# The last four gate and value tiles of blocks 3 to 8 as seven half-size products in place of eight

## The chip, the cores and the metric

The kernel runs on one core of one Trainium2 chip. The metric is the time of one execution on the device in microseconds (us). Executions of one kernel mostly agree within a few tenths of a per cent, so a ratio of two kernels is taken over several runs of each. One run of the kernel before, 349.77 us, is 1.6% above the fastest of its kernel, counts as slow and is left out of the ratio. A profile is one execution among these: its span is about 1.8 us shorter than the time reported for the same execution. Its opening (blocks 0 to 2 and the first loads) differs by up to 3 us. Parts of two profiles are therefore compared from block to block here, not by their spans.

## The reference

Two layers in a row. The first is a normed linear attention without softmax:

```
kv  = einsum('bhsd,bhse->bhde', k, v)          # batch 8, heads 8, rows 576, head size 64
out = einsum('bhsd,bhde->bhse', q, kv)
x   = out / sqrt(mean(out * out, -1) + 1e-6) * g_norm
```

The second is a gated feed-forward layer on the 4608 rows of x, each 512 wide:

```
h   = gelu(x @ w_gate) * (x @ w_val)           # 512 -> 1536
y   = x + sigmoid(x @ w_res) * (h @ w_out)     # 1536 -> 512
```

## The kernel before

Each batch of 576 rows gives a block of 512 rows, and the 64 rows left of each of the eight batches make the ninth block: blocks 0 to 8. While block m runs through the feed-forward layer, attention of batch m + 1 is slipped in between its tiles. Per block TensorE computes twelve pairs of tiles (gate and value, each four matmuls of 512 columns), then the residual gate, then the output product. The output product is already done as seven half-size products for eight (Strassen's scheme in Winograd's form), with the sums of `hid` (the h of the formulas) on VectorE; `wA` to `wF` are its accumulators. The order of instructions on each engine is set by this program.

The accumulators lie in PSUM, eight of 128x512 in fp32, called banks here, in two rings of four: `pmoe` for the feed-forward layer and `pattn` for attention.

```python
    pmoe = ctx.enter_context(tc.tile_pool(name="pmoe", bufs=4, space=bass.MemoryType.PSUM))
    pattn = ctx.enter_context(tc.tile_pool(name="pattn", bufs=4, space=bass.MemoryType.PSUM))
    ...
    def m_act(blk, f, gps, vps):
        ge = moep.tile([P, NJ * P], FP16, tag="ge", name="ge")
        nc.scalar.activation(out=ge, in_=gps, func=AF.Gelu)
        nc.vector.tensor_tensor(out=hids[blk][:, f, :], in0=ge, in1=vps, op=ALU.mult)
    ...
    def m_gval(blk, f, pool=pmoe, tag="mm"):
        ...
        gps = pool.tile([P, NJ * P], FP32, tag=tag, name="gps")
        m_mm(gps, wg_c, f, blk, 0, NJ)          # four matmuls of 512 columns
        vps = pool.tile([P, NJ * P], FP32, tag=tag, name="vps")
        m_mm(vps, wv_c, f, blk, 0, NJ)
        m_act(blk, f, gps, vps)
```

Attention's output `op` takes all four banks of `pattn`. ScalarE squares it, VectorE sums the squares (`a_ss`), then comes the norm (`a_norm`, twelve small instructions on VectorE: three refining steps of an inverse root), and `a_t` multiplies the four banks by it, which sets them free one by one:

```python
    def a_t(b, i):
        o, rinv = st[b]["o"][i], st[b]["rinv"]
        ...
        nc.vector.tensor_tensor(out=t, in0=o, in1=scale, op=ALU.mult)
```

Where these stand is set by numbers of tiles: `k0` for the product of keys and values, `o0` for the output, `n0` for the norm.

```python
        else:
            at(m - 1, NF, lambda: by_token(b, "q"))
            at(m - 1, NF + 1, lambda: by_token(b, "k"), *begin)
            k0, o0, n0 = 1, 3, 7
        at(m, k0, lambda: a_kv(b))
        ...
        at(m, o0, lambda: a_o(b))
        for j in range(NJ):
            at(m, o0 + j // 2, lambda j=j: a_ss(b, j))
        at(m, n0, lambda: a_norm(b, 0, NJ + rem))
        n0 += 1 if b == 2 else 2
        for j in range(NJ):
            at(m, NF if b == 2 and j > 1 else n0 + j // 2, lambda j=j: a_t(b, j))
```

## Time and profile before

| | before |
|---|---|
| time, median | 344.67 us (3 runs: 344.24, 344.67 and the slow 349.77) |
| span of the profile, of an execution of 347.15 us | 345.4 us |
| TensorE busy | 331.9 us, 96% |
| VectorE, ScalarE, GpSimd busy | 68%, 43%, 30% |
| waits of TensorE in blocks 3 to 8 | none listed |

The line of busy times says which engine is the bound; the list of waits of that engine says whether it loses anything to others. Here it loses next to nothing after the opening. The prediction below shows these lines and reads them.

### The profile page before, as it was taken

To read this page: it belongs to the slowest core of one execution; us is meant where nothing else is said; L and a number is where in the kernel's file an instruction comes from. 1 tells how busy PE (TensorE), PEld (TensorE's weight loads), DVE (VectorE), ACT (ScalarE), POOL (GpSimd) and SP (SyncE) were. 2 spreads that over 40 slices of the span, in tenths; PEclk is the share of its full clock that TensorE was granted. 3 is DMA by queue.
4 is the path that set the end of the run, shared out by engine and by line. 5 is a ranking of instruction groups with operands and counts; after the bars stand their busy time and mean duration, and the time that the engine had idled before them with its cause. 6 is when DMAs were issued, how large, how long until landed. Compare 5 with 4: busy or idle time off the path is not lost.

```text
span 345.4 us, 6165 instructions
## 1 busy us (share of the span) xinstructions
PE 331.9 (96%) x2432; PEld 188.0 (54%) x2432; DVE 236.5 (68%) x446; ACT 150.1 (43%) x265; POOL 103.1 (30%) x121
## 2 busy tenths in 40 slices
PE   8789999999899999999999999999999999999992
PEld 3544454445744475447544764476447644764481
DVE  5665549769859987698578976885688735453643
ACT  3573384274336352535263615361736133623350
POOL 2692161980064108200820083005000600050013
PEclk9899999999999999999999999999999999999997
DMA  7999999669589263966395439744003120030004
GB/s 244 290 178 204 195 204 166 168 95 150 117 108 164 94 123 120 165 60 128 130 167 43 102 114 174 79 92 153 17 0 61 63 76 2 1 121 4 0 2 121
DMA packets 76399, 38.81 MB, mean 112 GB/s; under 512 B 42066, under 2 KB 73810, under 8 KB 76370
## 3 DMA queue, kind: packets, MB, share of 16 engines
q0 software_dynamic: 38752, 17.17, 40.1%
q1 hardware_dynamic: 37184, 20.71, 21.6%
q10 hardware_dynamic: 434, 0.52, 0.5%
q8 instruction: 19, 0.31, 0.4%
q14 instruction: 10, 0.08, 0.1%
HBM read 38.80 MB, written 9.44 MB: 140 GB/s over the span
## 4 chain that ended last, share of the span: by engine, by line
PE 69%; DVE 2%; issue 0%; POOL 0%; POOLq 0%; DVEq 0%
PE gps L336 21%; PE vps L336 20%; PE wA L431 10%; PE rps L356 6%; PE wF L431 3%; PE wD L431 2%; PE w L431 2%; PE wE L431 2%; PE kvp L187 1%; PE op L205 1%; DVE t L282 1%; DVE hid L325 1%; DVE hid_s L404 0%; DVE t L296 0%; POOL osb L526 0%
## 5 line engine op out<-in xcount | busy, mean ns | idle before, releaser
L324 ACT ACTIVATE ge<-gps 128x512 f16<-128x512 f32 x108 | 64.3, 597 | 133.1 <-PE gps L336 127.8
L325 DVE TENSOR_TENSOR hid<-ge,vps 128x512 f16<-128x512 f16 x108 | 73.8, 684 | 63.2 <-PE vps L336 60.8
L336 PE MATMUL vps<-xT,wv 128*128 128x512 f16 x424 | 108.8, 379 | 0.4 <-DVE hid L325 0.4
L336 PE MATMUL gps<-xT,wg 128*128 128x512 f16 x424 | 109.0, 379 | 0.0
L470 POOL TENSOR_TENSOR osb<-osb,t 128x512 f32<-128x512 f32 x28 | 36.1, 1309 | 155.6 <-DVE osb L466 148.6
L336 PEld LDWEIGHTS <-wv 128*128 128x128 f16 x424 | 41.5, 98 | 50.6 <-issue 0.7
L336 PEld LDWEIGHTS <-wg 128*128 128x128 f16 x424 | 40.2, 98 | 45.4 <-issue 0.4
L431 PEld LDWEIGHTS <-hid_s 128*128 128x128 f16 x384 | 37.5, 98 | 6.3 <-issue 1.4
L356 PE MATMUL rps<-wr,xT 128*128 128x512 f16 x144 | 32.7, 379 | 0.0
L431 PEld LDWEIGHTS <-hid 128*128 128x128 f16 x288 | 28.2, 98 | 5.1
L365 ACT ACTIVATE th<-rps 128x512 f32<-128x512 f32 x36 | 21.5, 597 | 19.0 <-PE rps L356 19.0
L356 PEld LDWEIGHTS <-xT 128*128 128x128 f16 x144 | 14.1, 98 | 16.8
L224 DVE TENSOR_REDUCE ss<-sq 128x8 f32<-128x512 f32 x32 | 20.6, 679 | 2.9 <-ACT sq L222 2.7
L431 PE MATMUL wA<-wo_ts,hid_s 128*128 128x256 f16 x168 | 20.6, 273 | 1.2 <-DVE wF L404 1.2
L370 ACT ACTIVATE th<-th 128x512 f32<-128x512 f32 x36 | 19.9, 622 | 0.0
L282 DVE TENSOR_TENSOR t<-op,ny 128x512 f16<-128x512 f32 x28 | 17.9, 682 | 0.1
L222 ACT ACTIVATE sq<-op 128x512 f32<-128x512 f32 x28 | 15.3, 597 | 4.5 <-PE op L205 4.2
L296 DVE TENSOR_TENSOR t<-t,g 128x512 f16<-128x512 f16 x36 | 16.2, 498 | 0.1
L404 DVE TENSOR_TENSOR hid_s<-hid 128x1536 f16<-128x1536 f16 x16 | 15.3, 955 | 0.3
L526 POOL TENSOR_TENSOR osb<-osb,t 128x512 f32<-128x512 f32 (+1 forms) x4 | 4.3, 1078 | 27.8 <-DVE osb L522 27.8
L373 PE MATMUL fps<-wo,hid 128*128 128x512 f16 x48 | 11.2, 379 | 0.0
L431 PE MATMUL wD<-wo_ts,hid_s 128*128 128x256 f16 x84 | 10.3, 273 | 0.1
(133 smaller groups left out, 326.5 us busy)
## 6 DMA issues: line engine op xcount, KB each, us to landing
out_dram<-osb SPq DMA_DIRECT2D x14, 512.0 KB, 2.6
qraw<-in_q_dram POOLq DMA_DIRECT2D x7, 512.0 KB, 8.2
kraw<-in_k_dram POOLq DMA_DIRECT2D x7, 512.0 KB, 9.9
v<-in_v_dram POOLq DMA_DIRECT2D x7, 512.0 KB, 11.9
out_dram<-osb SPq DMA_DIRECT2D x5, 256.0 KB, 2.8
wg<-in_moe_w_gate_dram POOLq DMA_DIRECT2D x2, 512.0 KB, 9.2
wv<-in_moe_w_val_dram POOLq DMA_DIRECT2D x2, 512.0 KB, 9.4
wo<-in_moe_w_out_dram POOLq DMA_DIRECT2D x2, 512.0 KB, 14.2
```

Of the source, the lines that this page charges most:

```text
L222: nc.scalar.activation(out=sq, in_=src, func=AF.Square)
L224: nc.vector.tensor_reduce(out=out_, in_=sq, op=ALU.add, axis=mybir.AxisListType.X)
L282: nc.vector.tensor_tensor(out=t, in0=o, in1=scale, op=ALU.mult)
L296: nc.vector.tensor_tensor(out=t_t[blk][:, jj, :], in0=t_t[blk][:, jj, :], in1=g16, op=ALU.mult)
L324: nc.scalar.activation(out=ge, in_=gps, func=AF.Gelu)
L325: nc.vector.tensor_tensor(out=hids[blk][:, f, :], in0=ge, in1=vps, op=ALU.mult)
L336: nc.tensor.matmul(ps[:, j0 * P : j1 * P], lhsT=w[:, cc, :], rhs=xT_t[blk][:, j0:j1, cc, :], start=(cc == 0 and j0 == 0), stop=(cc == NP - ...
L356: nc.tensor.matmul(rps, lhsT=xT_t[blk][:, j, cc, :], rhs=wr16[:, cc, :], start=(cc == 0), stop=(cc == NP - 1),)
L365: nc.scalar.activation(out=th, in_=rps, func=AF.Tanh, scale=0.5)
L370: nc.scalar.activation(out=th, in_=th, func=AF.Copy, scale=0.5, bias=0.5)
L431: nc.tensor.matmul(ps[:, e - es[0], :], lhsT=a[:, f, e * P : (e + 1) * P], rhs=b[:, f, :], start=(start and e == es[0] and f == 0), stop=( ...
L470: nc.gpsimd.tensor_tensor(out=res_all[of], in0=res_all[of], in1=t_t[blk][of], op=ALU.add)
```

## The change

The intent: the last four pairs of tiles of a block, 512 rows by 512 deep by 512 columns for gate and for value, are done by the same scheme of seven half-size products in place of eight. TensorE is the bound, so an eighth of that part should be time saved. The two groups of 128 columns run side by side: for each, the accumulators `E` and `D` lie in `pmoe` and `A` in `pattn`, and the partial results set aside (`d`) in a buffer that is free at that time. The sums of the weights are taken once, in block 0, on VectorE; the sums of x per block on GpSimd. To clear attention's banks in time, the norm of batches 4 to 7 is moved from tile 7 to tile 5; the multiplication by g and one sum of `hid` move behind the products. Three buffers in SBUF were merged or cut to make room.

The core of the diff (cut):

```diff
+    def gval_by_products(blk):
+        ...
+        def prod_w(ps, g, a, b, start):
+            for n in range(2):                       # gate, value
+                for c in range(NP // 2):
+                    nc.tensor.matmul(ps[:, n, :], lhsT=a(n)[:, c, g * P : (g + 1) * P], rhs=b[:, :, c, :], ...)
+        def first():
+            for g in range(2):
+                w[g]["E"] = pmoe.tile([P, 2, PR], FP32, tag="mm", name="gE")
+                w[g]["D"] = pmoe.tile([P, 2, PR], FP32, tag="mm", name="gD")
+                w[g]["A"] = pattn.tile([P, 2, PR], FP32, tag="at", name="gA")
+                w[g]["d"] = th_all[:, g, :].rearrange("p (n t) -> p n t", n=2)
+                prod_w(w[g]["A"], g, wh(1, 1), x_of(blk, 1, 1), True)
+                nc.scalar.copy(out=w[g]["E"], in_=w[g]["A"])
+            for g in range(2):
+                prod_w(w[g]["D"], g, s_(1), x_sum[:, 0], True)
+                nc.scalar.copy(out=w[g]["d"], in_=w[g]["D"])
+        ... second, third, fourth: five more products, recombined by VectorE into D and c,
+        ... then gelu on ScalarE and the multiplication on VectorE (for c on GpSimd)
@@ plan_attn
-            k0, o0, n0 = 1, 3, 7
+            k0, o0, n0 = 1, 3, 5 if b > 3 else 7
-        n0 += 1 if b == 2 else 2
+        n0 += 1 if b != 3 else 2
-            at(m, NF if b == 2 else n0 + 1, lambda j=j: a_x(b, j))
+            at(m, n0 + 1 if b == 3 else NF, lambda j=j: a_x(b, j))
@@ blocks
+            if blk > 2:
+                slots[F0:] = gval_by_products(blk)
+                plan.setdefault(0, []).insert(0, lambda: x_sums(blk))
-            plan.setdefault(NFH + 2, []).insert(0, lambda: s_begin(blk))
+            if blk <= 2:
+                plan.setdefault(NFH + 2, []).insert(0, lambda: s_begin(blk))
             def products(blk=blk, outs=outs):
                 s_rest(blk)
+                if blk > 2:
+                    s_begin(blk)
```

## The prediction

> **What bounds the kernel now.** I read the page's busy shares first, then the costliest groups, then the waits of TensorE alone, and last the timelines of TensorE, VectorE and GpSimd over one steady block.
>
> From the page:
>
> ```profile
> PE 331.9 (96%) x2432; PEld 188.0 (54%) x2432; DVE 236.5 (68%) x446; ACT 150.1 (43%) x265; POOL 103.1 (30%) x121
> L325 DVE TENSOR_TENSOR hid<-ge,vps 128x512 f16<-128x512 f16 x108 | 73.8, 684 | 63.2 <-PE vps L336 60.8
> L282 DVE TENSOR_TENSOR t<-op,ny 128x512 f16<-128x512 f32 x28 | 17.9, 682 | 0.1
> ```
>
> TensorE (PE) is busy 96% of a 345.4 us span; the gate and value tiles wait almost only for it. All waits of TensorE that the profile lists are short, and none falls in blocks 3 to 8:
>
> ```profile
> PE kvp L718 <- DVE v L689: 2.5, 2, 2.3
> PE wA L431 <- DVE wF L404: 1.2, 1, 1.2
> PE vps L336 <- DVE hid L325: 0.4, 1, 0.4
> ```
>
> The windows of three such blocks show no idle time at all: 35.24, 34.86 and 34.50 us long, with PE busy for the whole of each at a granted clock of 1.00. So a us of products saved is a us of time saved, if nothing new makes TensorE wait. Its timeline in the block that starts at 201.64 us gives the rates (start, duration, columns as in the page; starts, not ends, tell the rate):
>
> ```profile
> 199.02 1.47 PE L431 MATMUL wF<-wo,hid_s 128*128 128x256 f16 x12
> 200.33 1.47 PE L431 MATMUL wA<-wo_ts,hid 128*128 128x256 f16 x12
> ...
> 211.81 1.03 PE L336 MATMUL gps<-xT,wg 128*128 128x512 f16 x4
> 212.67 1.03 PE L336 MATMUL vps<-xT,wv 128*128 128x512 f16 x4
> ...
> 216.99 1.03 PE L336 MATMUL gps<-xT,wg 128*128 128x512 f16 x4
> ...
> 223.89 2.32 PE L356 MATMUL rps<-wr,xT 128*128 128x512 f16 x10
> ```
>
> From 216.99 to 223.89 are the last four tile pairs: 32 matmuls of 512 columns in 6.90 us, 0.216 us each. Twelve of 256 columns start 1.31 us apart as a group (199.02 to 200.33), 0.109 us each. VectorE in the same block:
>
> ```profile
> 212.08 0.69 DVE L325 TENSOR_TENSOR hid<-ge,vps 128x512 f16<-128x512 f16 x1 [0.23 <-PE vps L336]
> 212.68 1.27 DVE L224 TENSOR_REDUCE ss<-sq 128x8 f32<-128x512 f32 x2
> 213.87 0.68 DVE L325 TENSOR_TENSOR hid<-ge,vps 128x512 f16<-128x512 f16 x1
> ...
> 217.86 0.17 DVE L254 TENSOR_SCALAR nm<-ss 128x32 f32<-128x32 f32 x1
> ...
> 220.10 0.19 DVE L262 SCALAR_TENSOR_TENSOR ny<-na,ny 128x32 f32<-128x32 f32 x1
> 220.21 0.68 DVE L325 TENSOR_TENSOR hid<-ge,vps 128x512 f16<-128x512 f16 x1
> ```
>
> The twelve small instructions of the norm take 220.21 - 217.86 = 2.35 us in a row, more than a pair of tiles on TensorE (1.73 us). Now that costs nothing: a late `hid` only holds a bank of a ring of four.
>
> **What the Trainium skill says.** "TensorE: Matmul & The Clock Gate", section "Wait — 56ns, not 53.3ns?", gives 215.7 ns from start to start at 512 columns, warm, as columns over 2.4 GHz plus 2.5 ns; for 256 that is an estimate of 109 ns. The trace has 216 and 109, so half-size products cost half and no more. "PSUM — Partial Sum Buffer", section "PSUM bank collisions raise a hardware error", says that two engines must not be in one bank and quadrant at once and that software has to guard it by semaphores; "Engine vs sequencer instructions" there says that VectorE's queue is strict FIFO. Together they are my main worry: a product may wait for a bank whose last reader sits behind the norm. The trace shows both: banks wait for `hid`, and VectorE keeps program order. "SBUF — State Buffer", section "Who interferes with whom", says that VectorE and GpSimd share a port pair as an exclusive lock, for a VectorE instruction with two SBUF inputs too. The trace agrees: one `t<-t,g` took 1.26 us at 203.42 beside a GpSimd addition, against four in 1.42 us at 190.46.
>
> **The change part by part.** Products: per block 32 x 0.216 = 6.90 us go, and 7 products x 2 groups x 4 matmuls = 56 x 0.109 = 6.12 us come: 0.78 us saved, 4.7 us over six blocks. That is the most it can give, 1.4%.
>
> Weight sums, once, in block 0: eight VectorE sums of 128x512 f16, about 0.34 us each (a 128x1536 one takes 0.955), 2.7 us. They delay the last `hid` of that block from 41.52 to about 43.1; its bank is wanted by the fourth residual product about 43.85. Hidden, narrowly.
>
> Token sums: four GpSimd sums at 1.3 us (the row of wo_ts) after the last block's additions, so from about 4.0 to 9.2 us of the block; wanted at 17. Hidden. The next loads are issued 5 us later, and have till about 30 us. Hidden.
>
> Pieces after the products (copies, recombining, gelus, multiplications): more instructions, half as large, on ScalarE (43% busy), VectorE and GpSimd. I laid them out by hand with 0.4 us for 256 columns and 0.69 for 512: once started, the fourteen group-products never wait longer than 0.2 us, since each bank is left for about 1.5 us between two uses.
>
> Start of the products: here I see the loss. The two `A` accumulators take attention's banks, whose last readers are the `t<-op,ny` multiplications. The order of instructions in the changed kernel shows two separate waits for VectorE in front of the two `A`; by rotation of four banks they are the first two `t`. The change brings the norm forward to behind tile 5, and the first two `t` behind tile 6. In the block above, by VectorE's own times: `hid` 5 at 213.87, norm from 214.47 to 216.82, `hid` 6, then the first `t` from 217.42 to 218.10. TensorE is ready at 216.99 and waits 1.15 us; the second `t` ends at 218.70 and costs 0.16 more. With the 6.12 us of products the phase ends near 224.4, against 223.89: 0.5 us worse than before. In blocks with remainder rows one more reduction (0.68 us) and a norm of 2.42 us come first: the first `t` ends near 184.0 where TensorE is ready at 182.13 in the block that starts at 166.40, a wait of 1.85 us, so 1.3 us worse. Blocks 3 and 5 are of the first kind, 4 and 6 of the second, and 7 and 8 have no attention, so they gain the full 0.75.
>
> End of the phase: the sums of `hid` for the output products begin about 1.8 us after the last product, as all four now come at the end, with the four `t<-t,g` and the next batch's two copies behind them. `wF<-wA,wd` then starts about 8.3 us after the last gate product, against 7.7 (196.67 - 189.01) before, and ends just after product E (8.7): a new wait of 0.1 to 0.4 us in blocks 3, 4 and 5, together 0.9. The transposed x of the next block is issued about 7.5 us after the phase, lands 4.3 us later (the trace's landing time) and is wanted at 12.6: hidden.
>
> Sum: 2 x 0.5 + 2 x 1.3 - 2 x 0.75 + 0.9 = +3.0 us, on 344.67: 347.7. VectorE may be a little quicker than laid out, and the change was made by someone who moved the norm on purpose, so I say 347.0.
>
> **The rivals.** First, the banks are free in time and the products save their 4.7 us: 340. For it: the norm was moved forward for just this, and blocks 7 and 8 have it. Against it: VectorE's timeline, where reductions, norm and two `hid` stand ahead of the first `t` with no idle time. Second, VectorE becomes the bound in the whole block (27.40 us of 34.86 now, some 1.5 us more): blocks grow by 1 to 2 us each at the end of the phase also, 350 to 352. Against it: 6 us idle remain. Third, GpSimd is late: its sums or its two multiplications are slowed by the shared port, or loads pushed back delay VectorE's copies; 349 or more. Against it: about 8 us of slack for the first sum, and GpSimd is 30% busy.
>
> **Range and chances.** The low end, 341.5, is nearly the full gain; the high end, 350.5, is twice my loss. Over 2% faster would need 337.8, beyond the most that the products can save. Over 2% slower needs 351.6, which takes the second rival in full.
>
> **What would show it.** Right: in blocks 3 to 6 the first `gA` waits 1 to 2 us for VectorE's `t`, longer in 4 and 6; the pieces within the phase run without gaps; blocks 7 and 8 are 0.75 us shorter; `wA` or `wF` of the output products waits a little for `wF<-wA,wd`. Wrong: no wait at the first `gA` (then 340), a wait for `x_sum` or the GpSimd `hid`, or 256-column products further apart than 0.11 us.

## The result, and the profile after

| | before | after |
|---|---|---|
| time, median of 4 runs each | 344.60 us (344.52 without the slow 349.77) | 348.06 us (347.30 to 348.77) |
| ratio, 95% interval | | 1.0104 (1.0075 to 1.0132) |
| TensorE busy | 331.9 us | 327.5 us |
| VectorE busy | 236.5 us | 251.2 us |
| GpSimd busy | 103.1 us | 137.5 us |

The output is correct.

TensorE has less work and the kernel is slower, by 1.0%. The page after, busy times:

```profile
PE 327.5 (95%) x2576; PEld 200.3 (58%) x2576; DVE 251.2 (73%) x490; ACT 164.9 (48%) x313; POOL 137.5 (40%) x157
```

The 4.4 us less of TensorE's busy time only look like what the products should save. From the residual products of block 2 to those of block 8 the busy time fell by 3.2 us, from 207.10 to 203.89; the rest is mostly in the opening, where the profile before had its 3.4 us at half the clock. The waits of TensorE in the changed kernel (in total, times, longest; those in the opening left out) say where the gain went:

```profile
PE gA L476 <- DVE t L283: 6.0, 4, 1.8
PE wA L432 <- DVE wF L405: 1.2, 1, 1.2
PE vps L337 <- DVE hid L326: 0.4, 1, 0.4
```

The last two were there before. The first is new: four waits of the first `gA` for `t`, attention's multiplication. Its 6.0 us against 3.2 us less of busy time make the 2.8 us that the blocks lose below. TensorE's timeline in block 5, which begins at 201.19 us, shows one; the brackets give the idle time ahead of an instruction and who ended it:

```profile
214.81 1.03 PE L337 MATMUL gps<-xT,wg 128*128 128x512 f16 x4
215.67 1.03 PE L337 MATMUL vps<-xT,wv 128*128 128x512 f16 x4
217.94 0.39 PE L476 MATMUL gA<-xT,wg 128*128 128x256 f16 x2 [1.24 <-DVE t L283]
218.17 0.38 PE L476 MATMUL gA<-xT,wv 128*128 128x256 f16 x2
218.53 0.39 PE L476 MATMUL gA<-xT,wg 128*128 128x256 f16 x2
...
221.60 1.04 PE L476 MATMUL gA<-x_sum,w_sum 128*128 128x256 f16 x8
222.47 1.04 PE L476 MATMUL gD<-xT,w_sum 128*128 128x256 f16 x8
...
224.22 3.62 PE L357 MATMUL rps<-wr,xT 128*128 128x512 f16 x16
```

Once begun, the products run without a gap that matters: eight matmuls of 256 columns every 0.87 us (221.60 to 222.47), 0.109 each. VectorE in the same stretch shows why they begin late:

```profile
213.42 0.68 DVE L326 TENSOR_TENSOR hid<-ge,vps 128x512 f16<-128x512 f16 x1
214.01 0.17 DVE L255 TENSOR_SCALAR nm<-ss 128x32 f32<-128x32 f32 x1
...
216.60 0.68 DVE L326 TENSOR_TENSOR hid<-ge,vps 128x512 f16<-128x512 f16 x1
217.20 1.28 DVE L283 TENSOR_TENSOR t<-op,ny 128x512 f16<-128x512 f32 x2
218.40 0.68 DVE L326 TENSOR_TENSOR hid<-ge,vps 128x512 f16<-128x512 f16 x1
```

VectorE has no idle time here: behind `hid` of tile 5 the norm takes 2.59 us, then `hid` of tile 6, then the first `t`, which ends about 217.88 (two of them take 1.28 us, one 0.68); `gA` follows at 217.94. TensorE had been ready since about 216.53, when the last plain tile was issued in full (215.67 and four times 0.216).

To compare whole blocks I take the time from the start of one block's residual products (`rps`) to the next block's, out of TensorE's timelines:

| interval ending at `rps` of block | 3 | 4 | 5 | 6 | 7 | 8 | sum |
|---|---|---|---|---|---|---|---|
| before | 35.20 | 35.23 | 34.88 | 35.24 | 33.34 | 33.35 | 207.24 |
| after | 35.95 | 36.63 | 35.73 | 36.64 | 32.55 | 32.55 | 210.05 |
| difference | +0.75 | +1.40 | +0.85 | +1.40 | -0.79 | -0.80 | +2.81 |

Blocks 7 and 8, without attention beside them, gain; blocks 3 to 6 lose, and those with remainder rows (4 and 6) lose most.

### The profile page after: what moved, and what is told of

Its sections match the earlier page's. It is cut to its first block, busy times and chain, and to the rows that moved or that the text cites. A ratio compares the mean times of both kernels' runs of the same rounds, so it can differ in the third digit from the quotient of the medians.

```text
span 345.5 us, 6641 instructions
## 1 busy us (share of the span) xinstructions
PE 327.5 (95%) x2576; PEld 200.3 (58%) x2576; DVE 251.2 (73%) x490; ACT 164.9 (48%) x313; POOL 137.5 (40%) x157
## 4 chain that ended last, share of the span: by engine, by line
PE 62%; DVE 9%; issue 2%; POOL 0%; POOLq 0%; DVEq 0%
PE gps L337 12%; PE vps L337 12%; PE wA L432 10%; PE gA L476 6%; PE rps L357 6%; PE gD L476 3%; PE wF L432 3%; DVE hid L326 2%; PE wD L432 2%; PE w L432 2%; PE wE L432 2%; PE gE L476 2%; DVE ss L225 2%; DVE t L283 1%; PE kvp L188 1%
## 5 line engine op out<-in xcount | busy, mean ns | idle before, releaser
L325 ACT ACTIVATE ge<-gps 128x512 f16<-128x512 f32 x84 | 50.0, 597 | 106.3 <-PE gps L337 105.5
L326 DVE TENSOR_TENSOR hid<-ge,vps 128x512 f16<-128x512 f16 x84 | 57.3, 685 | 48.8 <-PE vps L337 46.4
L337 PE MATMUL vps<-xT,wv 128*128 128x512 f16 x328 | 84.2, 379 | 0.4 <-DVE hid L326 0.4
L337 PE MATMUL gps<-xT,wg 128*128 128x512 f16 x328 | 84.3, 379 | 0.0
L337 PEld LDWEIGHTS <-wv 128*128 128x128 f16 x328 | 32.1, 98 | 39.3 <-issue 0.7
L337 PEld LDWEIGHTS <-wg 128*128 128x128 f16 x328 | 30.8, 98 | 34.1 <-issue 0.4
L498 POOL TENSOR_TENSOR hid<-ge,osb 128x256 f16<-128x256 f16 x12 | 8.0, 675 | 64.6 <-ACT ge L493 64.6
L476 PEld LDWEIGHTS <-w_sum 128*128 128x128 f16 x192 | 18.8, 98 | 2.2
L405 POOL TENSOR_TENSOR x_sum<-xT,x_sum 128x512 f16<-128x512 f16 x12 | 13.8, 1153 | 0.5
```

The source lines that it names most:

```text
L337: nc.tensor.matmul(ps[:, j0 * P : j1 * P], lhsT=w[:, cc, :], rhs=xT_t[blk][:, j0:j1, cc, :], start=(cc == 0 and j0 == 0), stop=(cc == NP - ...
L405: eng.tensor_tensor(out=out_, in0=in0, in1=in1, op=op)
L476: nc.tensor.matmul(ps[:, n, :], lhsT=a(n)[:, c, g * P : (g + 1) * P], rhs=b[:, :, c, :], start=(start and n == 0 and c == 0), stop=(c == N ...
```

## The experiments

The theory: the products save what they should, and VectorE's backlog of attention work at their start, on which the banks hang, takes more than that back. The rivals: the copies and sums around the products eat the gain; what was moved (late sums of `hid`, token sums on GpSimd) costs it; VectorE's total work has become the bound. Four kernels ran on one chip, then three on another, each set with its own runs of the kernel before (medians 344.76 and 344.47 us). In the first set (later norm, attention earlier, blocks 7 and 8, moves alone) two of the eleven runs of the kernel before took 348.6 and 348.9 us and count as fast; they lift its mean and so lower the ratios of that set by 0.001 to 0.002. All seven gave correct outputs, the one with the coarser norm included.

**The products where no attention runs.** The products in blocks 7 and 8 only; attention's plan and the other blocks as before the change.

```diff
-            k0, o0, n0 = 1, 3, 5 if b > 3 else 7
+            k0, o0, n0 = 1, 3, 7
-            if blk > 2:
+            if blk > 6:
                 slots[F0:] = gval_by_products(blk)
```

(The two lines below the first that place `a_t` and `a_x` are put back too, and `s_begin` follows the same bound. The weight sums and the merged buffers stay.)

> The products in blocks 7 and 8 alone, which have no attention beside them; attention's plan and the sums of the other blocks as before. Theory (half-size products save 0.78 us a block less some small change): 1.5 us less than before, 343.1, ratio 0.9957. Rival (the products save nothing once their copies and sums are paid): 344.6, ratio 1.000 or above.

Measured: 343.12 us, ratio 0.9941 (0.9902 to 0.9980). The intervals of blocks 7 and 8 are 32.55 us each, 0.8 less than before, and those of blocks 3 to 6 are as before within 0.01 us. The products do save their share, with their copies and sums paid.

**What was moved, without the products.**

```diff
             if blk > 2:
-                slots[F0:] = gval_by_products(blk)
                 plan.setdefault(0, []).insert(0, lambda: x_sums(blk))
```

> All that the change moves (norm and multiplications earlier, g multiplication and the sum of hid later, the weight and token sums, which nobody reads) but plain tiles in place of the products. Theory (the moves are hidden, the loss lies with the products' banks): 344.6 to 345.0, ratio 1.000 to 1.001, no wait of TensorE over 0.5 us in blocks 3 to 8. Rival (the late sums of hid or the GpSimd sums cost the time): 346 to 348.

Measured: 344.79 us, ratio 1.000 (0.9959 to 1.0040). Every interval of blocks 3 to 8 is that of before within 0.01 us. So neither the norm's new place, nor the late sums of `hid`, nor the weight and token sums cost anything by themselves in these blocks. That rival falls.

**The norm one tile later.**

```diff
-            k0, o0, n0 = 1, 3, 5 if b > 3 else 7
+            k0, o0, n0 = 1, 3, 6 if b > 3 else 7
```

> The changed kernel with the norm of batches 4 to 7 one tile later (behind tile 6, first multiplications behind tile 7). Theory (the wait is for the multiplications in VectorE's order): the first gA waits 1.3 us longer in blocks 3 and 5 and 0.85 us longer in 4 and 6, together 4.3, so 352.4, ratio 1.023. Rival (it waits for something else, so the norm's place is of no account): 348, ratio 1.010.

Measured: 354.08 us, ratio 1.0249 (1.0193 to 1.0305). The waits for `t` are 2.66 to 2.74 us each, 10.8 in all: 4.8 more than in the changed kernel, where 4.3 was expected. The time rose by 6.0. Part of the rest is something that I had not thought of, the clock: two of the four runs took 353.1 and 353.2 us at a mean granted clock of 0.991 and 0.996, the other two 355.0 us at 0.985, and the profile is of one of these. The windows of the products' phase of blocks 3 and 4 in this profile (us, then busy time and count of PE, PEld, DVE, ACT, POOL, then the granted clock of TensorE, and what the DMA engines did):

```profile
146.98:154.93 7.95, 7.95 (x56) 6.25 (x57) 5.17 (x9) 3.88 (x8) 0.70 (x2) 0.79 0.60 55
186.00:193.77 7.77, 7.54 (x56) 6.20 (x57) 5.28 (x10) 3.91 (x8) 0.70 (x2) 0.80 0.59 51
```

TensorE is busy nearly throughout, and still the 56 matmuls take 7.5 to 8 us in place of 6.3, at a clock of 0.79 and 0.80. In blocks 5 and 6 of the same profile, after waits as long, the clock stayed at 1.00. So such a wait sometimes brings a stretch of low clock; when, is read from the traces at the end of this section.

**A shorter norm.** One refining step in place of three for batches 4 to 7; the result is a little less exact on purpose.

```diff
-        for _ in range(3):
+        for _ in range(1 if b > 3 else 3):
             nc.vector.tensor_tensor(out=a, in0=yy, in1=yy, op=ALU.mult)
```

> The changed kernel with one refining step of the norm in place of three for batches 4 to 7 (so the output is less exact, on purpose): six small VectorE instructions less ahead of the multiplications, 1.3 to 1.4 us, every instruction else in its place. Theory (backlog): the first gA waits 1.3 us less in each of four blocks, so not at all in blocks 3 and 5 and 0.4 us in 4 and 6; 348.1 - 5.4 = 342.7, ratio 0.994. Rival (the wait is for the bank's place in the order, not for VectorE's time; or another engine takes over): 346 or more.

Measured: 342.12 us, ratio 0.9939 (0.9923 to 0.9955). The waits for `t` in the profile of this run:

```profile
PE gA L476 <- DVE t L283: 0.8, 2, 0.4
```

Two of 0.4 us are left, in blocks 4 and 6, as expected to the tenth. Nothing but VectorE's time ahead of `t` was changed, so that time is what TensorE waited for.

**Attention one tile earlier.**

```diff
-            k0, o0, n0 = 1, 3, 5 if b > 3 else 7
+            k0, o0, n0 = (0, 2, 4) if b > 3 else (1, 3, 7)
```

> The changed kernel with attention of batches 4 to 7 one tile earlier (key-value product behind tile 0, output behind tile 2, norm behind tile 4, first two multiplications behind tile 5), nothing else. Theory (the loss is the wait of the first gA for the bank that attention's multiplications hold): the four waits of 1.2 to 1.8 us and the 0.15 us at the second gA vanish, 6.6 us in all, so 348.1 - 6.6 = 341.5, ratio to before 0.991. Rival (VectorE has become the bound of these blocks, or the pieces after the products cost it): the wait moves elsewhere and the time stays at 346 to 348.

Measured: 346.26 us, ratio 1.0036 (0.9998 to 1.0073). A miss: 1.8 us gained where I expected 6.6. The waits of TensorE in this run:

```profile
PE gD L476 <- DVE hid L326: 4.5, 4, 1.2
PE gA L476 <- DVE t L283: 0.3, 1, 0.3
```

The wait at `gA` is all but gone, and the second `gD`, which takes the bank of the last plain tile, waits instead. VectorE and TensorE in block 3 of this run:

```profile
144.14 1.28 DVE L283 TENSOR_TENSOR t<-op,ny 128x512 f16<-128x512 f32 x2
145.34 0.68 DVE L326 TENSOR_TENSOR hid<-ge,vps 128x512 f16<-128x512 f16 x1
145.93 1.28 DVE L283 TENSOR_TENSOR t<-op,ny 128x512 f16<-128x512 f32 x2
147.13 0.67 DVE L326 TENSOR_TENSOR hid<-ge,vps 128x512 f16<-128x512 f16 x1
148.98 1.30 DVE L405 TENSOR_TENSOR gD<-gA,th 128x512 f32<-128x512 f32 x2 [1.18 <-issue]
```

```profile
146.19 0.60 PE L476 MATMUL gD<-x_sum,w_sum 128*128 128x256 f16 x4
147.86 0.60 PE L476 MATMUL gD<-x_sum,w_sum 128*128 128x256 f16 x4 [1.06 <-DVE hid L326]
```

VectorE is still more than a us behind: four `t` and two `hid` stand in a row, and the last `hid` ends at 147.80, just before the second `gD` runs. Then VectorE stands idle for 1.18 us. The view names no releaser; by the program's order the next thing VectorE is to do needs a product that TensorE does behind that `gD`. So my theory was too narrow: not the bank of `t` is the matter but the backlog, which comes out at whichever bank is wanted first.

**The third and fourth multiplication put into that idle time**, with attention one tile earlier as in the run before.

```diff
-            at(m, NF if b == 2 and j > 1 else n0 + j // 2, lambda j=j: a_t(b, j))
+            at(m, NF if b == 2 and j > 1 else n0 + j // 2 * (2 if b > 3 else 1), lambda j=j: a_t(b, j))
```

> The earlier run with attention one tile earlier showed the wait at gA gone and a new one of 1.1 us at the second gD, for the bank of the last plain hid, which VectorE reaches only after the third and fourth multiplication of attention. Here those two are put behind the next tile's hid as well. Theory (VectorE's backlog at the start of the products is the cost, whichever bank it shows at, and the two multiplications fit into VectorE's idle time behind it): the 4.5 us of waits at gD vanish too, about 346.3 - 4.7 = 341.6, ratio to before 0.991. Rival (the work of VectorE in these blocks is too much in total, and the wait moves to a third place such as gD<-gA or hid_s): 345 to 346.

Measured: 342.12 us, ratio 0.9934 (0.9921 to 0.9947). The list of waits has no `gD` any more, and of `gA` only this:

```profile
PE gA L476 <- DVE t L283: 0.3, 1, 0.3
```

VectorE in block 3 now has the two `hid` side by side and the last two `t` behind them:

```profile
142.68 1.28 DVE L283 TENSOR_TENSOR t<-op,ny 128x512 f16<-128x512 f32 x2
143.88 1.28 DVE L326 TENSOR_TENSOR hid<-ge,vps 128x512 f16<-128x512 f16 x2
145.07 1.28 DVE L283 TENSOR_TENSOR t<-op,ny 128x512 f16<-128x512 f32 x2
146.33 1.30 DVE L405 TENSOR_TENSOR gD<-gA,th 128x512 f32<-128x512 f32 x2
```

The intervals are 34.43, 35.40, 34.22, 35.21, 32.55 and 32.55 us. Blocks 3 and 5 have gained 0.77 and 0.66 us, nearly as much as 7 and 8; blocks 4 and 6 stand about where they were before the change. With remainder rows VectorE seems to be still a little late at the start of the products: from start to start, TensorE loses 0.15 to 0.4 us at each of four places ahead of `gA` and `gD` there. The first of these is the wait listed above; for the others the list names nobody. The rival that VectorE's total work is the bound falls: the same work in another order fits. This version beats both kernels.

**The later multiplications alone**, attention where the change has it: the same edit of that line on the changed kernel.

> The changed kernel with only the third and fourth multiplication put two tiles behind the first two, attention where the change has it. Theory: they stand behind the first two, for which gA waits, so the waits at gA stay at 1.2 and 1.8 us; 348.1, ratio 1.010. Rival (the room for the multiplications alone is what matters): 343 to 345.

Measured: 348.08 us, ratio 1.0106 (1.0085 to 1.0127). This run tells nothing apart: no instruction of VectorE is issued between the old and the new place, so the order on every engine came out the same as in the changed kernel. It is a repeat of it, and as such it shows two things. The ratio, 1.0104 then, holds. And its profile caught the clock effect in the changed kernel's own order. Windows in block 6, where `gA` waited from about 253.25 to 255.04 (columns as above):

```profile
256.60:258.00 1.40, 1.40 (x8) 0.97 (x7) 0.77 (x2) 1.35 (x3) 0.00 (x0) 0.50 0.02 6
258.00:259.90 1.90, 1.90 (x11) 1.32 (x9) 1.20 (x2) 0.22 (x1) 0.00 (x0) 0.50 0.04 9
259.90:262.99 3.09, 3.09 (x31) 2.73 (x29) 2.23 (x5) 1.60 (x5) 0.71 (x2) 1.00 0.00 0
```

For 3.4 us, beginning 1.45 us after the end of a wait of 1.79 us, the granted clock is 0.50, and the interval of block 6 is 38.31 us, 1.67 more than in the first profile of this order (36.64). Of four waits in that profile one had this effect, and in the first profile none.

The traces show what made the difference. In each of the nine, from the first record of the clock (7 to 10 us in) on, its changes lie a whole number of 3.413 us apart (with the later norm at 148.21, 151.62, 185.76 and 189.17 us). Cut into stretches of 3.413 us at these times, the traces have TensorE idle for 1.79 us in the stretch ahead of the fall in block 6 here:

```profile
253.07:256.49 3.42, 1.63 (x13) 1.09 (x13) 3.32 (x9) 0.47 (x1) 0.00 (x0) 1.00 0.00 0
```

In the first profile of this order the wait of 1.79 us in block 4 reached over the end of its stretch, which so had 1.67 us of idle time, and the next stretch stayed at 1.00:

```profile
178.68:182.09 3.41, 1.74 (x9) 0.59 (x6) 3.14 (x14) 0.60 (x1) 0.00 (x0) 1.00 1.45 198
182.09:185.51 3.42, 3.30 (x29) 2.74 (x30) 3.14 (x7) 2.13 (x4) 0.00 (x0) 1.00 1.67 163
```

The stretches ahead of the other falls, those after the last matmul apart, had 2.18 and 2.27 us (later norm, blocks 3 and 4) and 2.29 and 2.12 us (the openings of the profile before and of the moves alone) of idle time. The waits of 2.7 us in blocks 5 and 6 of the later norm were parted by the end of a stretch, with 1.33 to 1.38 us on each side, and nothing fell. So in these traces the clock fell when TensorE had been idle for more than about half of a stretch, and a wait of 1.8 us costs 1.7 us more or nothing, by where it lies.

## Why the prediction was right

The time came out at 348.06 us for 347.0 predicted, within the range, and the sum worked out in the text before it was shaded, 347.7, was nearer. The mechanism is the one predicted; that the sum fits so closely is in part luck, as two of its terms were off in opposite directions. By its steps:

- **The bound.** Right. Where nothing makes TensorE wait, fewer products are less time: 0.8 us a block in the run with blocks 7 and 8 alone.
- **The saving, 0.78 us a block.** Right: -0.79 and -0.80 in blocks 7 and 8. The estimate of 109 ns for 256 columns, from "TensorE: Matmul & The Clock Gate", section "Wait — 56ns, not 53.3ns?", and the trace agree: 0.109 us.
- **The start of the products.** Right in kind: TensorE waits for VectorE's first two `t`, behind norm and `hid`. Counted as the prediction counts, from when the last plain tile is issued in full, the first `gA` is 1.4 us late in blocks 3 and 5 and 1.95 in 4 and 6, for 1.15 and 1.85 predicted (the bracketed 1.2 and 1.8 us begin only at the modelled end of the matmuls), and the second `gA` 0.15 more, for 0.16. So the phase came out a little worse than predicted in blocks 3 and 5: from the block's start to `rps` 23.03 us against 22.25 before, +0.8 for +0.5. Most of that is the norm, 2.59 us for 2.35: two of its instructions took 0.42 and 0.35 us where the profile before has 0.18 and 0.17. GpSimd was issuing a load then; whether that is the cause, I did not test. The step to correct is what I took the wait to be: I saw a wait for a bank of attention. The earlier-attention run showed a backlog of VectorE that the next bank inherits.
- **The end of the phase, 0.9 us in all.** Too large. A wait that fits `wF<-wA,wd` is there, too short to be listed, and it is 0.07 us: product E (`wE`) starts 1.38 us before the next `wA` in blocks 3 to 5, in place of 1.31, and `wF<-wA,wd` ends about 0.05 us before that `wA` begins (232.94 and 232.99). VectorE began the sums of `hid` about as laid out, 1.75 us after the last product (225.97 - 224.22), and reached `wF` at 8.03 (232.25) rather than 8.3. So the sum of the parts is right by two errors that cancel: 0.3 us too little for the start in two blocks and 0.7 too much for the end.
- **The sum.** +3.0 us predicted, +2.81 in the profiles from block to block; the lost starts (7.3 us in all) and the end (0.2) less the products' 4.7 give the same. The times differ by 3.5 (348.06 against 344.52). The clock explains only part of the 0.7 us left. The profiles with one slow stretch have a mean granted clock of 0.990 to 0.992, those with none 0.993 to 0.997; of the four runs of the changed kernel one, 348.77 us at 0.990, fits a slow stretch, and the others, 347.30, 347.90 and 348.22 us at 0.994 to 0.996, do not. Why two of these three are 0.6 and 0.9 us longer than the profiled one stays open; the opening is where profiles differ most, but these runs have none.
- **The hidden parts.** Weight sums, token sums, later loads, the transposed x: all hidden, as the run with the moves alone shows; no wait for them is listed in blocks 3 to 8 of the changed kernel either. The weight sums took 0.42 us each where 0.34 was predicted.
- **The rivals.** The first (no wait) is what blocks 7 and 8 do. The second (VectorE as the bound) fell with the run that only reorders it. The third (GpSimd late) never showed; no wait for `x_sum` is listed.

## What to carry to other kernels

Before giving the bounding engine less work, look at the order of the engine that frees its buffers just where the new work begins: in this kernel a ring of four banks absorbed a late consumer, and a phase that takes six of the eight banks at its start did not. A first wait that is taken away may come back at the next buffer if the engine behind it is still late; so move work out from between, not only forward. And an idle us of TensorE can cost more than itself, when its clock drops after it: here 1.7 us after a wait of 1.8.

## What the Trainium skill lacked or had wrong

- "TensorE: Matmul & The Clock Gate", section "What's actually happening", has the clock fall to half after at least one idle window of about 3.4 us, and "HAM oscillation — how this bites in real kernels" warns of idle gaps over about 3.4 us. Here a gap of 1.79 us sufficed: granted clock 0.50 for 3.4 us after it, 1.67 us lost; gaps of 2.7 us had it in two of four blocks, of 1.8 us in one of four. So shorter gaps count too: in these traces, whenever 1.79 us or more of a stretch of 3.413 us was idle (five cases), and never at 1.67 us or less.
- No page says, beyond general advice to have enough buffers and to empty PSUM promptly, that a product phase that takes six of eight banks of PSUM at its start turns a consumer's backlog, hidden before, into waits of the bounding engine (6.0 us here), or that the wait moves from bank to bank (from `gA`, 6.0 us, to `gD`, 4.5 us). "PSUM — Partial Sum Buffer" has the rule for sharing a bank only as one of correctness.
